# A different order of steps around the values of an attention kernel, with two of three key tiles of exponentials added on VectorE ahead of the sums

## The chip, the cores and the metric

The kernel runs on one core of one Trainium2 chip. The metric is the device time of one execution in microseconds (us), as the median of several executions. Every run also reports the core's span (first to last instruction; the quoted time is 1.8 us more in most runs, up to 3 in some) and the mean clock that was granted to TensorE, as a share of full speed. Engines are named as in the profile: PE is TensorE, PEld its weight loads, DVE is VectorE, ACT is ScalarE, POOL is GpSimd.

## The reference

A grouped-query attention (8 batches, 16 query heads on 4 key/value heads, 384 positions, head size 64) feeds a gated feed-forward layer whose gate is mixed over the positions:

```python
k, v = repeat(k, 4), repeat(v, 4)                  # 4 query heads share one key/value head
attn = exp(q @ k.T / 8 - max); attn = attn / attn.sum(-1)
x    = (attn @ v) -> [8, 384, 1024]
h    = maximum(x @ w_in, 0)                        # w_in [1024, 1024]
u, v = h[..., :512], h[..., 512:]
v_n  = (v - mean(v)) / sqrt(var(v) + 1e-6)
v_s  = einsum('ts,bsd->btd', w_spatial, v_n) + b_spatial
out  = (u * v_s) @ w_out                           # w_out [512, 1024]
```

## The kernel before

A batch is cut into small steps. The order in which the program issues them is the order in which each engine works. I use these short names, which are also those of the new code: `s` scores of one pair of PSUM banks (two matmuls of 512 columns), `e` their exps on ACT, `m` the sums of the exps (matmuls against a block of ones), `r` a reciprocal on ACT (`Ln`, then `Exp` of the negative), `x` the values (attention times v), `n` their normalisation on DVE, `V` the gate's v half with its relu on DVE, `S` its statistics on DVE, `rs` and `vn` the layer norm on ACT and DVE, `p` the mix over positions, `U` the u half with the gating on DVE, `O` one out chunk, copied out of PSUM by DVE. A prime counts batches back: `O0''` is an out chunk of two batches ago. `C0` and `C1` are the two values steps of a batch: 2 sums, 2 reciprocals, 4 values, 4 normalisations each. "Burst s9" below is the group of three score pairs s9, s10, s11, and so on.

PSUM has eight banks, and the one that was freed longest ago is taken next. A score burst needs three pairs, so six of the eight:

```python
    def take1():
        x = min((i for i in range(8) if not busy[i]), key=lambda i: used[i])
        ...
    def take2():
        x = min((i for i in range(0, 8, 2) if not busy[i] and not busy[i + 1]),
                key=lambda i: (max(used[i], used[i + 1]), min(used[i], used[i + 1])))
        ...
    def tiles(dst, a, quad, weights):
        for t in range(NST):                       # 3 key tiles
            for i in range(4):                     # 4 column groups of 32
                half, j = i // 2, quad * 2 + i % 2
                nc.tensor.matmul(dst[32 * i : 32 * (i + 1), :], weights(t, half),
                                 a[:, t, half, j * S : (j + 1) * S],
                                 start=(t == 0), stop=(t == NST - 1))

    def sums(b, gp, quad):
        x = take1()
        tiles(f32(x, S), T["aT", b, gp], quad, lambda t, half: ones32)
        T["sum", b, gp, quad] = x

    def norm(b, gp, quad, jj):
        ...
        nc.vector.tensor_tensor(T["xT", b][:, gp * 4 + quad * 2 + jj, :],
                                f32(x, S), T["rec", b, gp, quad], ALU.mult)
        touch(x)                                   # the bank is free after this

    def project(b, i, split=1):                    # O: one out chunk
        ...
        x = take1()
        pe_group(banks[:, x, :], ...)              # 4 matmuls
        nc.vector.tensor_copy(osb[:, half * 512 : (half + 1) * 512], banks[:, x, :])
        touch(x)
```

The steady order is made of six visits per batch:

```python
    def visit(b, vi):
        us = [3 * vi, 3 * vi + 1, 3 * vi + 2]
        ...                                        # score(u) x3, expo(u) for the first two
        if vi == 1 and b > 1:
            C(b - 1, 1, (0, 1))
        if vi == 4 and b < B:
            C(b, 0, (0, 1))
        ...                                        # expo of the third
        f, g = b - 1, b - 2
        run(*{
            0: [("sp", g, 2), ("U", g, 2), ("sp", g, 3), ("U", g, 3)],
            1: [("O", g, 0)],
            2: [("V", f, 0), ("st", f, 0), ("O", g, 1), ("V", f, 1), ("st", f, 1)],
            3: [("O", g, 2), ("V", f, 2), ("st", f, 2), ("O", g, 3), ("rs", f, 0), ("vn", f, 0)],
            4: [("O", g, 4)],
            5: [("O", g, 5), ("sp", f, 0), ("U", f, 0), ("sp", f, 1), ("U", f, 1)],
        }[vi])
        ...                                        # loads, casts and turns of the next batch
```

The softmax here doesn't subtract the row's maximum and nothing guards it: scores larger than these inputs give would overflow.

Of the kernel before, what the change touches and what calls it, by code (L numbers as in the profile page):

```python
# [17 lines left out]
def kernel(  # L18
# [73 lines left out]
    def take2():  # L92
        x = min(
            (i for i in range(0, 8, 2) if not busy[i] and not busy[i + 1]),
            key=lambda i: (max(used[i], used[i + 1]), min(used[i], used[i + 1])),
        )
        mark(True, (x, x + 1))
        return x
# [162 lines left out]
    def score(b, u):  # L261
# [3 lines left out]
        x = take2()  # L265
        rhs = T["qT", b, gp].rearrange("p j t q -> p (j t q)")
        for half in range(2):
            lo, hi = half * D, (half + 1) * D
            nc.tensor.matmul(  # L269
                banks[:, x + half, :],  # L270
# [5 lines left out]
        T["sc", b, u] = x  # L276

    def expo(b, u):
        gp, c, t = u // 9, (u % 9) // 3, u % 3
        x = T["sc", b, u]  # L280
        nc.scalar.activation(  # L281
            T["aT", b, gp][:, t, :, c * 512 : (c + 1) * 512], banks[:, x : x + 2, :], AF.Exp, scale=scale
        )
        touch(x, x + 1)

    def tiles(dst, a, quad, weights):
        for t in range(NST):
            for i in range(4):
# [3 lines left out]
                    weights(t, half),  # L292
                    a[:, t, half, j * S : (j + 1) * S],
                    start=(t == 0),
                    stop=(t == NST - 1),
                )

    def sums(b, gp, quad):
        x = take1()
        tiles(f32(x, S), T["aT", b, gp], quad, lambda t, half: ones32)  # L300
# [10 lines left out]
    def value(b, gp, quad, jj):  # L311
        v16 = T["v16", b]
# [3 lines left out]
            T["aT", b, gp],  # L316
            quad,
            lambda t, half: v16[:, 2 * gp + half, t, 32 * jj : 32 * (jj + 1)],
# [29 lines left out]
    def v_half(b, st):  # L348
        x = v_mm(b, st, range(4))
        part = ff.tile([P, DH], FP32, name=f"vpart_{st}", tag=f"vpart_{st}", bufs=1)  # L350
# [4 lines left out]
    def u_half(b, mu):  # L355
        x = u_mm(b, mu, range(4))
        part = ff.tile([P, S], FP32, name=f"upart_{mu}", tag=f"upart_{mu}", bufs=1)
# [4 lines left out]
    def gate_v(b, st):  # L362
# [3 lines left out]
        if part is None:  # L366
            if V_ON_ACT:
                nc.scalar.activation(v_r, banks[:, x, :], AF.Relu)
            else:
                nc.vector.tensor_scalar(v_r, banks[:, x, :], 0.0, None, op0=ALU.max)  # L370
# [86 lines left out]
    V_ON_ACT = False  # L457

    def ff_item(it):
        kind, b, i = it  # L460
        if b < 0 or b >= B:
            return
        {
            "V": gate_v, "st": stats, "sp": spatial, "U": gate_u, "O": project,
            "VA": v_half, "UA": u_half,
            "rs": lambda b, i: rstd(b), "vn": lambda b, i: v_norm(b, nc.vector),
        }[kind](b, i)


    def run(*items):  # L470
        for it in items:
            ff_item(it)

    def C(b, gp, quads):
        for qd in quads:
            sums(b, gp, qd)
        for qd in quads:
            recip(b, gp, qd)
        for qd in quads:
            for jj in range(2):  # L480
                value(b, gp, qd, jj)
                norm(b, gp, qd, jj)

    def visit(b, vi):
        us = [3 * vi, 3 * vi + 1, 3 * vi + 2]
        done = b == 1 and vi == 0
        if b < B and not done:
            for u in us:
                score(b, u)
            for u in us[:2]:  # L490
                expo(b, u)
        if vi == 1 and b > 1:
            C(b - 1, 1, (0, 1))
        if vi == 4 and b < B:
            C(b, 0, (0, 1))
        if b < B and not done:
            expo(b, us[2])
        f, g = b - 1, b - 2
        run(*{
            0: [("sp", g, 2), ("U", g, 2), ("sp", g, 3), ("U", g, 3)],  # L500
            1: [("O", g, 0)],
            2: [("V", f, 0), ("st", f, 0), ("O", g, 1), ("V", f, 1), ("st", f, 1)],
            3: [("O", g, 2), ("V", f, 2), ("st", f, 2), ("O", g, 3), ("rs", f, 0), ("vn", f, 0)],
            4: [("O", g, 4)],
            5: [("O", g, 5), ("sp", f, 0), ("U", f, 0), ("sp", f, 1), ("U", f, 1)],
        }[vi])
        n = b + 1
        if 2 <= n < B:
            if vi == 0:
                load_k(n)  # L510
                load_q(n, 0)
                load_v(n)
                load_q(n, 1)
            if vi == 1:
                cast_k(n, pool)
                for qd in range(2):
                    cast_q(n, 0, pool, 0, qd)
                    cast_q(n, 0, pool, 1, qd)
            if vi == 2:
                turn_k_dma(n)  # L520
                turn_q_dma(n, 0)
                for qd in range(2):
                    cast_q(n, 1, pool, 0, qd)
                    cast_q(n, 1, pool, 1, qd)
                cast_v(n, pool)
            if vi == 3:
                turn_q_dma(n, 1)

    with tc.manual_schedule():
        load_k(0, (0,))  # L530
        load_q(0, 0, (0,))
        load_q(0, 0, (1,))
        load_v(0)
        load_k(0, (1,))
        load_q(0, 1, (0,))
        load_q(0, 1, (1,))
# [4 lines left out]

        cast_k(0, vec, (0,))
        cast_q(0, 0, vec, 0, 0)
        cast_q(0, 0, pool, 1, 0)
        turn_k_pe(0, 0, act)
        turn_q_pe(0, 0, (0,), vec)
# [93 lines left out]
        for b in range(1, B):  # L640
            for vi in range(6):
                visit(b, vi)
# [39 lines left out]
```

## Time and profile before

| | before |
|---|---|
| median of the 3 runs known before the prediction | 272.46 us |
| the profiled run | 271.68 us, span 269.9 us, clock 1.00 |
| one steady batch (period) | 30.35 us, of which DVE works 18.1 and ACT 21.0 |

The prediction shows the lines that carry the argument. One view is added here, the waits of before (who waited on which line for whom: total us, times, longest):

```profile
ACT aT L281 <- PE banks L269: 44.2, 27, 3.0
DVE xT L326 <- ACT rec L308: 31.3, 17, 2.7
...
ACT rstd L388 <- DVE mv L384: 24.1, 8, 10.6
...
PE banks L290 <- ACT aT L281: 3.1, 7, 1.8
```

ACT waits for scores, DVE waits for reciprocals, and ACT waits for V2's statistics before `rs`. Idle time of an engine that is not the busiest costs nothing by itself, but it can make something late that PE needs, such as the normalisations, whose banks the next burst takes. Only the last line is a wait of PE, the engine that is nearly always busy. It is small because most of PE's waiting hides inside groups that the profile counts as busy. That is why all sizes below are differences of starts: a burst's start to the start of the next group, 0.75 us when undisturbed; what exceeds 0.75 I call its loss.

### The profile page before, as it was taken

The page shows a single profiled execution, that of the slowest core. Times are in us where ns is not written, and L with a number is a line of the kernel's source. Part 1 is how long each engine was busy: PE and PEld are TensorE (multiplying, and loading weights), DVE is VectorE, ACT ScalarE, POOL GpSimd, SP SyncE. Part 2 cuts the span into 40 slices and gives each one's busy share as a digit, 9 for nine tenths or more (in the row PEclk, how much of TensorE's full clock was granted, in tenths as well). Part 3 has the DMA queues.
Part 4 walks back from the last instruction along what each step waited for, and adds up shares of the span by engine and source line. Part 5 has one row for each costly group of instructions (what it writes and reads, how often), then busy time and mean ns, then how long its engine had stood idle before and what let it go on. Part 6 is the DMA issues. An engine that isn't in the chain of part 4 may idle for free.

```text
span 269.9 us, 5476 instructions
## 1 busy us (share of the span) xinstructions
PE 251.7 (93%) x2236; PEld 115.6 (43%) x2236; DVE 160.6 (60%) x309; ACT 171.2 (63%) x227; POOL 53.6 (20%) x100
## 2 busy tenths in 40 slices
PE   1799987799999999999999999999999999999994
PEld 1242432354345444454345444454345444454451
DVE  2424638685765466645765466635765566667964
ACT  2877987988495766577495766577595866520000
POOL 3639605343002500043002500043000000000000
PEclk9999999999999999999999999999999999999999
DMA  7999999890678529590868529490651021200415
GB/s 213 251 309 285 169 179 296 149 323 10 165 138 265 165 87 175 131 330 12 169 136 263 167 87 188 120 334 9 165 138 78 1 80 78 80 0 2 167 66 233
DMA packets 56921, 41.93 MB, mean 155 GB/s; under 512 B 26305, under 2 KB 53057, under 8 KB 56897
## 3 DMA queue, kind: packets, MB, share of 16 engines
q1 hardware_dynamic: 54048, 38.44, 52.6%
q0 software_dynamic: 2848, 3.15, 7.5%
q8 instruction: 17, 0.28, 0.5%
q14 instruction: 8, 0.06, 0.1%
HBM read 25.95 MB, written 12.58 MB: 143 GB/s over the span
## 4 chain that ended last, share of the span: by engine, by line
PE 73%; ACT 11%; DVE 10%; issue 3%; DMA 1%; POOL 0%; SPq 0%; DVEq 0%
PE banks L109 49%; PE banks L269 12%; PE banks L290 10%; ACT aT L281 6%; DVE xT L326 4%; DVE bn L383 2%; PE banks L250 2%; ACT rec L308 2%; DVE v_r L370 2%; DMA q<-in_q_dram 1%; ACT rec L306 1%; ACT rstd L388 1%; DVE v_r L372 1%; DVE mv L384 1%; ACT rstd L389 1%
## 5 line engine op out<-in xcount | busy, mean ns | idle before, releaser
L281 ACT ACTIVATE aT<-banks 128x1024 f16<-128x1024 f32 x144 | 137.8, 1023 | 44.7 <-PE banks L269 44.2
L269 PE MATMUL banks<-qT,kT 64*128 64x512 f16 x288 | 50.3, 393 | 3.5 <-ACT aT L281 1.0
L326 DVE TENSOR_TENSOR xT<-banks,rec 128x384 f16<-128x384 f32 x64 | 31.6, 552 | 33.3 <-ACT rec L308 31.3
L109 PE MATMUL banks<-w_out,gT 128*128 128x512 f16 x192 | 48.6, 380 | 0.0
L109 PE MATMUL banks<-xT,w_in 128*128 128x384 f16 x256 | 47.4, 326 | 0.0
L109 PE MATMUL banks<-w_in,xT 128*128 128x512 f16 x192 | 46.0, 380 | 1.2 <-DVE xT L326 0.6
L290 PE MATMUL banks<-aT,v 128*32 128x384 f16 x768 | 35.4, 332 | 3.1 <-ACT aT L281 3.1
L446 DVE COPY osb<-banks 128x512 f32<-128x512 f32 x48 | 32.5, 680 | 8.2 <-PE banks L109 8.1
L200 POOL CAST q<-q 128x384 f16<-128x384 f32 x57 | 28.0, 521 | 22.9 <-DMA q<-in_q_dram 20.7
L109 PEld LDWEIGHTS <-w_in 128*128 128x128 f16 x256 | 24.6, 98 | 17.1 <-issue 1.2
L109 PEld LDWEIGHTS <-xT 128*128 128x128 f16 x192 | 17.9, 98 | 25.4 <-issue 4.2
L290 PEld LDWEIGHTS <-v 128*32 128x32 f16 x768 | 22.1, 98 | 14.4 <-issue 5.8
L109 PEld LDWEIGHTS <-gT 128*128 128x128 f16 x192 | 16.7, 98 | 26.3 <-issue 8.9
L370 DVE TENSOR_SCALAR v_r<-banks 128x512 f32<-128x512 f32 x21 | 14.5, 692 | 22.0 <-PE banks L109 21.1
L269 PEld LDWEIGHTS <-kT 64*128 64x128 f16 x288 | 12.4, 94 | 35.0 <-issue 30.4
L176 POOL CAST k<-k 128x768 f16<-128x768 f32 x7 | 5.8, 827 | 108.4 <-DMA k<-in_k_dram 103.0
L427 DVE SCALAR_TENSOR_TENSOR gT<-banks,vs 128x384 f16<-128x384 f32 x28 | 15.6, 558 | 18.8 <-PE banks L109 18.8
L290 PE MATMUL banks<-aT,ones 128*32 128x384 f16 x384 | 20.6, 334 | 0.6
L109 PE MATMUL banks<-wsT,v_n 128*128 128x384 f16 x96 | 20.9, 327 | 0.0
L414 DVE TENSOR_TENSOR vs<-banks,bias_tp 128x384 f32<-128x384 f32 x32 | 17.6, 552 | 5.2 <-PE banks L109 4.8
L306 ACT ACTIVATE rec<-banks 128x384 f32<-128x384 f32 x32 | 15.5, 485 | 6.0 <-DVE vs L414 5.5
L388 ACT ACTIVATE rstd<-mv,eps_t 128x3 f32<-128x3 f32 x8 | 2.4, 297 | 24.1 <-DVE mv L384 24.1
(38 smaller groups left out, 123.9 us busy)
## 6 DMA issues: line engine op xcount, KB each, us to landing
q<-in_q_dram SPq DMA_DIRECT2D x32, 384.0 KB, 6.7
out_dram<-osb SPq DMA_DIRECT2D x23, 512.0 KB, 2.9
v<-in_v_dram SPq DMA_DIRECT2D x8, 384.0 KB, 5.9
k<-in_k_dram SPq DMA_DIRECT2D x7, 384.0 KB, 4.1
w_in<-in_moe_w_in_dram POOLq DMA_DIRECT2D x16, 128.0 KB, 6.0
w_out<-in_moe_w_out_dram POOLq DMA_DIRECT2D x2, 512.0 KB, 8.6
ws<-in_moe_w_spatial_dram SPq DMA_DIRECT2D x1, 576.0 KB, 8.7
out_dram<-osb SPq DMA_DIRECT2D x2, 256.0 KB, 2.4
```

Source lines behind the costliest of these rows:

```text
L109: nc.tensor.matmul(dst, w, m, start=(i == 0), stop=(i == n - 1))
L176: engine(T["k16", b][:, :, g0:g1, :], T["k32", b][:, g0:g1, :].rearrange("p g (t d) -> p t g d", t=NST),)
L200: engine(T["q16", b, gp][:, 2 * qd : 2 * qd + 2, :, half, :], T["q32", b, gp][:, qd, 2 * half : 2 * half + 2, :].rearrange("p j (t d) -> p ...
L269: nc.tensor.matmul(banks[:, x + half, :], T["kT", b][lo:hi, t, gp, :], rhs[lo:hi, c * 512 : (c + 1) * 512], start=True, stop=True,)
L281: nc.scalar.activation(T["aT", b, gp][:, t, :, c * 512 : (c + 1) * 512], banks[:, x : x + 2, :], AF.Exp, scale=scale)
L290: nc.tensor.matmul(dst[32 * i : 32 * (i + 1), :], weights(t, half), a[:, t, half, j * S : (j + 1) * S], start=(t == 0), stop=(t == NST - 1),)
L306: nc.scalar.activation(rec, f32(x, S), AF.Ln)
L326: nc.vector.tensor_tensor(T["xT", b][:, gp * 4 + quad * 2 + jj, :], f32(x, S), T["rec", b, gp, quad], ALU.mult)
L370: nc.vector.tensor_scalar(v_r, banks[:, x, :], 0.0, None, op0=ALU.max)
L414: nc.vector.tensor_tensor(vs, f32(x, S), bias_tp, ALU.add)
L427: nc.vector.scalar_tensor_tensor(T["gT", b][:, mu, :], src, 0.0, T["vs", b, mu], op0=ALU.max, op1=ALU.mult)
L446: nc.vector.tensor_copy(osb[:, half * 512 : (half + 1) * 512], banks[:, x, :])
```

## The change

The intent: two out chunks stand ahead of each values step, so that the exps and banks which the sums and values need are ready. The order ahead of C1 and C0 thus is burst, two out chunks, values step, burst. All four mix/gate steps `p U` of a batch stand in the two visits behind C0. And DVE adds two of the three key tiles of exps (fp16) before the sums, so that a sum streams two operands in place of three through PE. The adds are issued only from batch 2 on. The diff, cut to its core (the start-up is the same order in the new notation; buffers of partial results are merged so that the new tile `sT` has room):

```diff
+    def add(b, gp, c):
+        aT = T["aT", b, gp]
+        ...
+        cs = slice(c * 512, (c + 1) * 512)
+        nc.vector.tensor_tensor(T["sT", b, gp][:, :, cs], aT[:, 0, :, cs], aT[:, 1, :, cs], ALU.add)
+
     def sums(b, gp, quad):
         x = take1()
-        tiles(f32(x, S), T["aT", b, gp], quad, lambda t, half: ones32)
+        aT, sT = T["aT", b, gp], T.get(("sT", b, gp))
+        parts = [aT[:, t] for t in range(NST)] if sT is None else [sT, aT[:, 2]]
+        tiles(f32(x, S), quad, [(ones32, a) for a in parts])
...
-    def visit(b, vi):
-    ...
+    C1 = "m10' m11' r10' r11' x100' n100' x101' n101' x110' n110' x111' n111'"
+    C0 = "m00 m01 r00 r01 x000 n000 x001 n001 x010 n010 x011 n011"
+    VISITS = [
+        "s0 s1 s2 e0 e1 e2 a12' O0'' O1'' lk+ lq0+ lv+ lq1+", C1,
+        "s3 s4 s5 e3 e4 e5 V0' S0' V1' S1' a00 a01 ck+ cq0+",
+        "s6 s7 s8 e6 e7 e8 V2' S2' O2'' O3'' tk+ tq0+ cq1+ cv+",
+        "s9 s10 s11 e9 e10 e11 a02 O4'' rs' O5'' vn' tq1+", C0,
+        "s12 s13 s14 e12 e13 e14 p0' U0' p1' U1' a10",
+        "s15 s16 s17 e15 e16 e17 p2' U2' p3' U3' a11",
+    ]
...
+        for b in range(2, B):
+            play(b, STEADY if b > 2 else " ".join(w for w in STEADY.split() if w != "a12'"))
+        play(B, LAST)
```

`a` is an add, `l` a load, `c` a cast on POOL, `t` a turn (transposition) by DMA, and a plus counts batches ahead. In the same notation the order before was:

```text
s0 s1 s2 e0 e1 e2 p2'' U2'' p3'' U3''
s3 s4 s5 e3 e4 C1 e5 O0''
s6 s7 s8 e6 e7 e8 V0' S0' O1'' V1' S1'
s9 s10 s11 e9 e10 e11 O2'' V2' S2' O3'' rs' vn'
s12 s13 s14 e12 e13 C0 e14 O4''
s15 s16 s17 e15 e16 e17 O5'' p0' U0' p1' U1'
```

## The prediction

> **What bounds the kernel now.** I read the page first (engine shares, then slices), then the windows of one batch, then its timeline on TensorE (PE), then VectorE (DVE) around the places where PE stands still.
>
> From the page: PE is busy almost throughout, no other engine is close, and the granted clock is full, so the span is PE's time plus PE's holes.
>
> ```profile
> PE 251.7 (93%) x2236; PEld 115.6 (43%) x2236; DVE 160.6 (60%) x309; ACT 171.2 (63%) x227; POOL 53.6 (20%) x100
> ```
>
> The windows of three steady batches show a repeating period of 30.35 us. DVE works 18.1 us of it and ScalarE (ACT) 21.0 us:
>
> ```profile
> 109.40:139.75 30.35, 29.94 (x273) 13.80 (x272) 17.99 (x35) 21.00 (x29) 5.43 (x10) 1.00 0.65 169
> 139.75:170.10 30.35, 29.95 (x272) 13.80 (x272) 18.09 (x35) 21.00 (x29) 5.43 (x10) 1.00 0.65 163
> 170.10:200.46 30.36, 29.95 (x272) 13.77 (x272) 18.10 (x35) 21.01 (x29) 5.43 (x10) 1.00 0.59 163
> ```
>
> "Busy" hides waiting inside a group, so I take starts, not durations, from PE's timeline (start, length, engine, line, operation):
>
> ```profile
> 149.25 0.82 PE L269 MATMUL banks<-qT,kT 64*128 64x512 f16 x6
> 150.00 1.16 PE L290 MATMUL banks<-aT,ones 128*32 128x384 f16 x24
> 150.99 2.12 PE L290 MATMUL banks<-aT,v 128*32 128x384 f16 x48
> 153.04 1.04 PE L109 MATMUL banks<-w_out,gT 128*128 128x512 f16 x4
> 154.01 1.18 PE L269 MATMUL banks<-qT,kT 64*128 64x512 f16 x6
> 155.12 1.90 PE L109 MATMUL banks<-w_in,xT 128*128 128x512 f16 x8
> ...
> 164.61 1.44 PE L290 MATMUL banks<-aT,ones 128*32 128x384 f16 x24
> 166.27 2.13 PE L290 MATMUL banks<-aT,v 128*32 128x384 f16 x48 [0.22 <-ACT aT L281]
> 168.33 1.04 PE L109 MATMUL banks<-w_out,gT 128*128 128x512 f16 x4
> 169.30 1.39 PE L269 MATMUL banks<-qT,kT 64*128 64x512 f16 x6
> 170.62 0.60 PE L109 MATMUL banks<-w_out,gT 128*128 128x512 f16 x2
> ```
>
> An undisturbed score burst takes 150.00-149.25 = 0.75 us. The burst right after a values step takes 155.12-154.01 = 1.11 or 170.62-169.30 = 1.32, though one out chunk lies between. The sums take 0.99 us undisturbed, but 166.27-164.61 = 1.66 when the exps that they read (and the banks of the values) are late. So a batch loses 0.36+0.57+0.67 = 1.6 us of 30.35 to three stalls. Everything else, started one after the other, is 28.75 us of issue.
>
> The stalls are PSUM banks: the burst's third pair starts only when the last normalisation (xT, four at a 0.49 us pitch) is out.
>
> ```profile
> 168.09 1.96 DVE L326 TENSOR_TENSOR xT<-banks,rec 128x384 f16<-128x384 f32 x4 [1.30 <-ACT rec L308]
> 170.11 0.10 PEld L269 LDWEIGHTS <-kT 64*128 64x128 f16 x2 [0.37 <-issue]
> ```
>
> 168.09+1.96 = 170.05, and the last two weight loads follow at 170.11. The next group starts 0.57 us after that normalisation ends.
>
> **What the Trainium skill says.** "VectorE: DVE Perf Modes", section on the perf-mode tier table: tensor_tensor with all operands 16-bit in SBUF gets two elements a cycle, with a PSUM or fp32 operand one; the errata section there gives (N+151)/0.96 ns. The trace agrees at one per cycle: 384 elements give 557 ns by it, measured 552. The new add (1024 fp16 elements, all SBUF) has no row in the trace, so I estimate (512+151)/0.96 = 690 ns from that page; successive DVE operations start about 0.06 us before the former's recorded end (norms: 552 ns long, 0.49 pitch), so 0.63 us each.
> "TensorEngine Tiling (Array Packing)", Key Properties: a change of tiling mode drains the array. The trace shows about 0.1 us at each: an out chunk takes 0.87 us before another 128-column group and 0.97 before a score burst.
> "SBUF — State Buffer", Who interferes with whom: a DVE op with two SBUF inputs and a GpSimd op that reads SBUF exclude each other. No row of before shows it for tensor_tensor.
>
> **The change part by part.** The ramp is the same order. Only from batch 2 on are adds issued, so batches 0 and 1 keep three streams per sum.
>
> 1. *Sums.* Per batch four sums of 12 matmuls become 8. 24 take 0.99 us, so 16 take 0.66: 2 x 0.33 = 0.66 us less per batch, on the path. The total is 24 sums x 4 = 96 matmuls, and the built kernels do differ by 192 PE rows (matmul and weight load).
>
> 2. *Adds.* Six of about 0.63 us per batch, 36 in all: 3.8 us more DVE work per batch, 18.1 to 21.9 of about 29. DVE does not become the bound, but it becomes tight locally.
>
> 3. *Order.* There were 14 mode changes per batch (six score bursts, two values steps) and there still are. Only the pairs differ (out to values, values to scores), so I book nothing. Unstalled, the period is 28.75-0.66 = 28.1 us. The old stalls go: two out chunks (0.87+0.96) let three exps end (0.92 pitch) before the values need their banks, and the score burst after C1 needs n101 at 5.7 us and has it at 5.35.
>
> 4. *New stalls.* I walked one batch by hand from the start of its first burst, with trace durations (PE to DVE 0.2 us; relu with statistics 1.55; copy 0.66; norm and v_n 0.49) and the banks that the least-recently-used rule gives.
> - Burst s9 to s11: the third pair takes the banks of V2 and O2. V2 ends on PE at 12.1. DVE has relu and statistics of V1 from 9.75 to 11.3, adds a00 and a01 to 12.56, V2 with statistics to 14.1, O2's copy to 14.78. PE wants the pair at 14.33. With the 0.57 us of restart, the next group starts at 15.35 instead of 14.66: 0.69 us lost, most of it owed to the two adds.
> - C0 then starts at 17.2. DVE has a02, O4, O5 (to 18.06), v_n x3 (to 19.5), then the norms at 20.0, 20.5, 21.0, 21.5. Burst s12 to s14 starts at 19.9, and its third pair needs the second norm, 20.5: the next group comes at 21.08 instead of 20.64, 0.44 us lost. p0 and U0 then find their banks free within 0.05.
> - ACT ends the last exp of each burst before PE wants the bank everywhere; I find at least 1 us of slack except at the reciprocals of C0, about 0.1.
> Together 1.13 us, so the period is 28.1+1.1 = 29.2 us, against 30.35.
>
> 5. *Edges.* Before, batch 2's first burst starts at 55.1, the tail (after the last burst's sp and U) at 235.8, and the span ends at 269.9: 180.7 + 34.1. After: batch 1 now holds also p2 U2 p3 U3 of batch 0 in half form (4 x about 0.57 = 2.3 us), but it waits on exps (PE idles 1.82 us at 48.5, and ACT waits 1.85 us for statistics at 47.0). With V2 moved ahead of the third burst both shrink; I walk it to 54.5 instead of 55.1. Batches 2 to 7 are 6 x 29.2 + 0.3 (batch 2 has one values step without adds) = 175.5. The tail loses the gates moved out (3.6 us) and 0.33, and gains about 1 us, because only three out chunks (2.6 us), not four and more, cover the chain from V2's statistics over rstd to v_n: 31.1. Sum 54.5+175.5+31.1 = 261.1 us of span, 8.8 less than 269.9, so 272.46-8.8 = 263.7 us.
>
> **The rivals.**
> - *DVE takes the place of the wait.* If the adds ran at one element a cycle (1.22 us), DVE would gain 3.5 us a batch more, the s11 stall would grow by 1.1 and C0's chain by about 0.5: period 30.8, gain gone, about 272. For: the two stalls in my walk are both DVE's, and POOL casts can hold an add up for up to 0.5 us (the casts fall 4 to 13 us after a load's issue, which brushes a02). Against: fp16, unit stride, SBUF on all three sides.
> - *No new stall.* If DVE's queue is shorter than I booked, only PE's work is left: 28.1 a batch, 257 us. Against: DVE's order is fixed, and V2's and O2's evictions stand behind two adds.
> - *Only the matmuls count.* If the new order merely exchanged stalls one for one, 24 sums x 0.165 = 4.0 us would be all: 268.5.
> - *ACT binds.* 21.0 us of 29.2 with no queueing in my walk; only if reciprocals in C0 slip does s13 wait. A few tenths a batch.
>
> **Range and chances.** 263.7 us; each 0.3 us per batch of missed stall is 1.8 us in six batches. The no-new-stall rival sets the low side (257, unlikely), the one-for-one exchange the high side (268.5). I take 259.0 to 268.5. The 2% border is 267.0, which needs about 0.55 us a batch beyond my walk. Faster by over 2%: 0.80; within 2%: 0.18; slower: 0.02.
>
> **What would show it.** PE matmul count down by 96; the ones groups 16 long, 0.66 us. A period between 28.8 and 29.7. Six DVE adds a batch near 0.69 us each (1.2 would mean I am wrong on the mode). The bursts before O4 and after C0 longer than 0.75 us with the third pair's loads late, after osb's copy and after xT's norm. No stall in the first sums of C1. Batch 2's first burst near 54.5. I am wrong if the period is under 28.5 or the stalls sit in front of an exp.

## More of the kernel before

ACT's timeline around C0, in the batch whose PE lines the prediction shows:

```profile
164.77 0.30 ACT L388 ACTIVATE rstd<-mv,eps_t 128x3 f32<-128x3 f32 x1 [1.94 <-DVE mv L384]
165.10 0.20 ACT L389 ACTIVATE rstd<-rstd 128x3 f32<-128x3 f32 x1
165.21 1.92 ACT L281 ACTIVATE aT<-banks 128x1024 f16<-128x1024 f32 x2
```

The burst ahead of C0 starts at 163.86, but its exps start only at 165.21, since `rs` stands ahead of them and ACT was idle for 1.94 us before it. The values of C0, which need the banks of these exps, start at 166.27.

## The result, and the profile after

| | before | after |
|---|---|---|
| median (lowest to highest of 4 runs) | 272.22 us (271.84 to 272.48) | 262.01 us (261.42 to 264.03) |
| ratio, 95% interval | 1 | 0.9639 (0.9585 to 0.9693) |
| the profiled run | 271.68 us, span 269.9 | 262.19 us, span 260.4 |

The outputs are correct. A ratio here and below is the mean time of one kernel's runs over the mean of the other's of the same rounds, so it is not quite the ratio of the medians in the table. Executions over 1.5% slower than the fastest of the same kernel are left out of the means.

The page of the changed kernel, its engine line and the group of the adds (busy us, mean ns; then idle time before them):

```profile
PE 242.8 (93%) x2140; PEld 110.8 (43%) x2140; DVE 186.5 (72%) x345; ACT 172.6 (66%) x227; POOL 58.4 (22%) x100
...
L304 DVE TENSOR_TENSOR sT<-aT 128x1024 f16<-128x1024 f16 x36 | 26.6, 765 | 0.0
```

PE has 96 matmuls fewer, DVE 36 adds more. PE's share stays at 93%: the span shrank with its work. The mean of an add, 765 ns, hides a wide spread: the shortest took 657 ns, the median 683, the longest 1315.

Waits of the changed kernel:

```profile
DVE xT L338 <- ACT rec L318: 12.3, 10, 2.7
...
PE banks L269 <- DVE osb L459: 2.0, 4, 1.0
```

The normalisations wait 12.3 us in all for reciprocals where they waited 31.3. PE's wait for exps ahead of sums and values is gone from the list. In its place stands a wait of the scores for the copy of an out chunk.

Three batches in the view of windows (length, then busy us with instruction count of PE, PEld, DVE, ACT, POOL, the granted clock, DMA share, GB/s):

```profile
84.58:113.25 28.67, 28.58 (x258) 13.09 (x258) 21.84 (x40) 21.14 (x28) 6.26 (x10) 1.00 0.65 173
113.25:142.30 29.05, 28.52 (x257) 13.06 (x257) 22.47 (x40) 21.24 (x28) 6.67 (x10) 1.00 0.68 171
171.17:200.76 29.59, 28.54 (x257) 13.08 (x256) 22.92 (x40) 21.24 (x28) 5.91 (x10) 1.00 0.63 168
```

Unlike before, the batches differ: 28.67, 29.05 and 29.59 us for the same instructions. DVE's busy time grows along with the period, 21.84 to 22.92, at an equal count, so its instructions were stretched.

PE in the first of these batches (timeline: start, length, engine, line, operation):

```profile
98.50 1.17 PE L269 MATMUL banks<-qT,kT 64*128 64x512 f16 x6
99.60 1.90 PE L109 MATMUL banks<-w_out,gT 128*128 128x512 f16 x8
101.43 0.35 PE L291 MATMUL banks<-sT,ones 128*32 128x384 f16 x4
...
102.09 2.12 PE L291 MATMUL banks<-aT,v 128*32 128x384 f16 x48
104.15 0.91 PE L269 MATMUL banks<-qT,kT 64*128 64x512 f16 x6
105.14 0.65 PE L109 MATMUL banks<-wsT,v_n 128*128 128x384 f16 x3
```

The two sums take 102.09-101.43 = 0.66 us, without a hole before the values. Burst s9 takes 99.60-98.50 = 1.10 (a loss of 0.35), the burst after C0 105.14-104.15 = 0.99 (0.24). That was batch 3 (batches are counted from 0; the windows above are batches 3, 4 and 6). In batch 6 burst s9 looks so:

```profile
185.10 0.82 PE L269 MATMUL banks<-qT,kT 64*128 64x512 f16 x5
186.87 0.37 PE L269 MATMUL banks<-qT,kT 64*128 64x512 f16 x1 [0.96 <-DVE osb L459]
187.18 0.60 PE L109 MATMUL banks<-w_out,gT 128*128 128x512 f16 x2
```

It takes 187.18-185.10 = 2.08, a loss of 1.33. Its sixth matmul waits for the bank of O2, which DVE copies out. DVE's timeline in batch 3 (first line) and then in batch 6 shows what came ahead of that copy:

```profile
95.85 1.26 DVE L304 TENSOR_TENSOR sT<-aT 128x1024 f16<-128x1024 f16 x2
...
182.44 1.89 DVE L304 TENSOR_TENSOR sT<-aT 128x1024 f16<-128x1024 f16 x2
184.26 0.68 DVE L383 TENSOR_SCALAR v_r<-banks 128x512 f32<-128x512 f32 x1
...
186.13 1.29 DVE L459 COPY osb<-banks 128x512 f32<-128x512 f32 x2 [0.25 <-PE banks L269]
```

The same pair of adds, a00 and a01, took 1.26 us in one batch and 1.89 in the other. POOL's timeline at that moment of batch 6 (the second line is the second of the two casts alone), and then of batch 3:

```profile
182.38 1.42 POOL L200 CAST q<-q 128x384 f16<-128x384 f32 x2 [0.16 <-DMA q<-in_q_dram]
182.83 0.97 POOL L200 CAST q<-q 128x384 f16<-128x384 f32 x1
...
96.46 1.01 POOL L200 CAST q<-q 128x384 f16<-128x384 f32 x1 [0.69 <-DMA q<-in_q_dram]
```

Casts of q lie beside the adds in both batches, and whichever instruction starts later is stretched. In batch 6 the first cast began ahead of the adds and took its usual 0.51 us; the second began during the first add and took 0.97. In batch 3 the adds began first (95.85 and 96.42) and kept 0.66 and 0.68 us; the cast took 1.01. The whole trace agrees. The 21 adds with no cast beside them took at most 0.69 us, and so did the 3 that began ahead of the cast that they met. The 11 adds of 0.72 to 1.31 us all began while a cast ran, and each ended 0.54 us after the last such cast. (One more began 0.13 us before the end of a cast and kept 0.68 us.) Each cast of q that began during an add ended 0.37 us after that add. Over the batches the loss of burst s9 follows the length of the pair:

| batch | 2 | 3 | 4 | 5 | 6 | 7 |
|---|---|---|---|---|---|---|
| period, us | 29.56 | 28.67 | 29.05 | 28.87 | 29.59 | 28.59 |
| a00 and a01 together, us | 1.63 | 1.26 | 1.75 | 1.56 | 1.89 | 1.26 |
| loss of burst s9, us | 0.70 | 0.35 | 0.84 | 0.65 | 1.33 | 0.35 |
| loss of the burst after C0, us | 0.14 | 0.24 | 0.15 | 0.14 | 0.18 | 0.25 |

In all batches but 6, each 0.1 us that the pair is longer is about 0.1 us more loss (0.49 us longer and 0.49 more lost in batch 4 than in batch 3). Batch 6 lost 0.35 more than that, of which 0.25 is the wait of the copy in the last DVE line; why the copy waited there I could not find. The same copy waits in batch 6 of after_again and of e6, so it is not chance.

### The profile page after: what moved, and what is told of

Read it like the earlier page. It is cut to its first block, busy times and chain, and to the rows that moved or that the text cites. A ratio compares the mean times of both kernels' runs of the same rounds, so it can differ in the third digit from the quotient of the medians.

```text
span 260.4 us, 5301 instructions
## 1 busy us (share of the span) xinstructions
PE 242.8 (93%) x2140; PEld 110.8 (43%) x2140; DVE 186.5 (72%) x345; ACT 172.6 (66%) x227; POOL 58.4 (22%) x100
## 4 chain that ended last, share of the span: by engine, by line
PE 67%; DVE 18%; DMA 4%; ACT 4%; issue 3%; SPq 2%; POOL 0%; DVEq 0%
PE banks L109 46%; PE banks L269 10%; PE banks L291 9%; DMA q<-in_q_dram 4%; DVE xT L338 4%; DVE v_n L407 3%; DVE osb L459 3%; ACT aT L281 3%; PE banks L250 2%; DVE sT L304 2%; DVE bn L396 1%; DVE v_r L383 1%; DVE vs L427 1%; DVE uparts L438 1%; SPq L170 1%
## 5 line engine op out<-in xcount | busy, mean ns | idle before, releaser
L269 PE MATMUL banks<-qT,kT 64*128 64x512 f16 x288 | 46.7, 393 | 5.7 <-DVE osb L459 2.0
L109 PE MATMUL banks<-w_out,gT 128*128 128x512 f16 x192 | 45.7, 380 | 0.1
L109 PE MATMUL banks<-w_in,xT 128*128 128x512 f16 x192 | 45.1, 380 | 0.7 <-DVE xT L338 0.6
L338 DVE TENSOR_TENSOR xT<-banks,rec 128x384 f16<-128x384 f32 x64 | 31.4, 549 | 14.3 <-ACT rec L318 12.3
L200 POOL CAST q<-q 128x384 f16<-128x384 f32 x57 | 31.8, 587 | 16.3 <-DMA q<-in_q_dram 12.7
L109 PEld LDWEIGHTS <-gT 128*128 128x128 f16 x192 | 17.5, 98 | 29.8 <-issue 9.3
L304 DVE TENSOR_TENSOR sT<-aT 128x1024 f16<-128x1024 f16 x36 | 26.6, 765 | 0.0
L291 PEld LDWEIGHTS <-v 128*32 128x32 f16 x768 | 21.1, 99 | 11.0 <-issue 0.9
L383 DVE TENSOR_SCALAR v_r<-banks 128x512 f32<-128x512 f32 x21 | 14.4, 688 | 12.9 <-PE banks L109 12.3
L269 PEld LDWEIGHTS <-kT 64*128 64x128 f16 x288 | 10.9, 95 | 28.9 <-issue 23.1
L318 ACT ACTIVATE rec<-rec 128x384 f32<-128x384 f32 x32 | 16.7, 523 | 1.0
```

The costliest lines, as they stand in the source:

```text
L109: nc.tensor.matmul(dst, w, m, start=(i == 0), stop=(i == n - 1))
L200: engine(T["q16", b, gp][:, 2 * qd : 2 * qd + 2, :, half, :], T["q32", b, gp][:, qd, 2 * half : 2 * half + 2, :].rearrange("p j (t d) -> p ...
L269: nc.tensor.matmul(banks[:, xs[half], :], T["kT", b][lo:hi, t, gp, :], rhs[lo:hi, c * 512 : (c + 1) * 512], start=True, stop=True,)
L291: nc.tensor.matmul(dst[32 * i : 32 * (i + 1), :], weights if len(weights.shape) == 2 else weights[:, half, :], a[:, half, j * S : (j + 1) ...
L304: nc.vector.tensor_tensor(T["sT", b, gp][:, :, cs], aT[:, 0, :, cs], aT[:, 1, :, cs], ALU.add)
L318: nc.scalar.activation(rec, rec, AF.Exp, scale=-1.0)
```

## The experiments

All outputs were correct. Each kernel ran four times (a profile and three timed rounds) beside the kernel before on the same chip. The theory going in: the order gives most of the gain, the adds' 0.66 us a batch is eaten by stalls that they cause themselves on DVE. The rivals: the saved matmuls are the gain; or what limits is something other than DVE's queue. A remark that holds for all: the granted clock of many runs is about 0.99 since it dips for one to three fortieths of the span, most often during the start-up. In e3 such runs are longer by about 1.3 us and in e1 by 1.6 to 2.2; in the kernel before they are not (271.67 us at 0.993, 271.71 at 0.999 on one chip). So differences of less than about 2 us between kernels are read from the batches in the traces.

### e1: the new order without adds

```diff
     def play(b, text):
         for word in text.split():
             kind = word.rstrip("'+")
+            if kind[0] == "a":
+                continue
```

> The new order without any add; every sum again has three streams. My theory: the order alone already gives nearly all of the gain, because what the adds save on PE (0.66 us a batch) they give back at the third score pair of burst s9 to s11, where the profile of the changed kernel shows 0.35 to 1.33 us lost (mean 0.70 in batches 3 to 7). Without adds that loss falls to about 0.1 and the one after C0 from 0.19 to 0.1, so the period is 28.95+0.66-0.70 = 28.9 us and the time about 262 us, the same as with adds within 1 us (ratio to before 0.96). Rival (the adds' 96 matmuls come on top of the order's gain): 262+4 = 266 us, ratio 0.977.

Measured: 263.65 us (261.79 to 264.01), ratio 0.9667 (0.9629 to 0.9706). A batch took 29.00 us. PE at burst s9:

```profile
100.08 1.03 PE L269 MATMUL banks<-qT,kT 64*128 64x512 f16 x6
101.04 0.82 PE L109 MATMUL banks<-w_out,gT 128*128 128x512 f16 x3
```

The loss is 101.04-100.08-0.75 = 0.21, and 0.06 after C0. With the adds the means of batches 3 to 7 are 0.70 and 0.19. So the adds cost 0.62 us of new loss for 0.66 us of matmuls saved: 28.95 against 29.00 us a batch. In time the interval of e1 overlaps that of the full change: by the ratios the adds are worth 0.8 or 1.1 us (the change was measured twice), by the medians 1.6 or 1.8. But three of e1's four runs had the clock dip; its one run at 1.00 took 261.79 us, and the change's runs at 1.00 took 261.42 to 262.19. The order is nearly all of the gain, and "only the matmuls count" is wrong.

### e2 and e2b: the adds in the old order

In e2 the old order was played with the adds put in, and a02 stood behind `vn'` (only the new lines are shown):

```diff
+        "s0 s1 s2 e0 e1 e2 p2'' U2'' p3'' U3'' a12' ...",
+        "s3 s4 s5 e3 e4", C1, "e5 O0'' a00 ...",
+        "s6 s7 s8 e6 e7 e8 V0' S0' O1'' V1' S1' a01 ...",
+        "s9 s10 s11 e9 e10 e11 O2'' V2' S2' O3'' rs' vn' a02 ...",
+        "s12 s13 s14 e12 e13", C0, "e14 O4'' a10",
+        "s15 s16 s17 e15 e16 e17 O5'' p0' U0' p1' U1' a11",
```

> The old order with the same 36 adds, each put where VectorE is idle; 96 matmuls fewer. My theory: in the old order both values steps are followed by a wait on ScalarE (exps, then reciprocals, then norms), so PE only waits 0.33 us longer after each shorter sum: 271 to 272.5 us, no gain to speak of. Rival (the matmuls lie on the path wherever they are): 272.2-4.0 = 268.2 us, ratio 0.985.

Measured: 281.88 us (280.80 to 282.76), ratio 1.0349 (1.0316 to 1.0382). The waits of this kernel name the reason:

```profile
PE banks L291 <- DVE sT L304: 15.4, 9, 2.3
```

PE waited 15.4 us for the sums' new operand. The layer norm `vn'` waits for ACT behind three exps, and my a02 stood behind it in DVE's queue. This was my bad placement, and the run says nothing about adds in the old order. e2b moves the three adds to where DVE is idle (a12' behind `p2''`, a01 ahead of `V0'`, a02 between `O2''` and `V2'`):

```diff
-        "s0 ... p2'' U2'' p3'' U3'' a12' ...",     "... V0' S0' O1'' V1' S1' a01 ...",     "... O2'' V2' S2' O3'' rs' vn' a02 ...",
+        "s0 ... p2'' a12' U2'' p3'' U3'' ...",     "... a01 V0' S0' O1'' V1' S1' ...",     "... O2'' a02 V2' S2' O3'' rs' vn' ...",
```

> The old order with the adds once more, now each where VectorE had idle time in the profile of the kernel before: in the first try a02 stood behind v_n, which waits for rstd behind the exps, and PE waited 15.4 us for the adds over the run. Only the three adds a01, a02 and a12 have moved. My theory: 96 matmuls fewer in the old order buy next to nothing, since PE waits for exps and norms after each values step: 271 to 272.5 us. Rival (they lie on the path): 268.2 us.

Measured: 272.47 us (272.11 to 272.98), ratio 1.0004 (0.9969 to 1.0040): the same as before, though the 96 matmuls are gone here as well. A batch takes about 30.36 us, as before. PE's timeline at C0:

```profile
134.71 0.35 PE L291 MATMUL banks<-sT,ones 128*32 128x384 f16 x4
...
136.37 0.83 PE L291 MATMUL banks<-aT,v 128*32 128x384 f16 x16 [0.38 <-ACT aT L281]
```

From the sums to the values it is 136.37-134.71 = 1.66 us, exactly the 1.66 of before, although the sums themselves became 0.33 us shorter. Burst s6 behind C1 took 1.33 us where it took 1.11. Where the exps or the normalisations set the moment at which PE may go on, shorter sums only make PE wait longer. So the adds are worth nothing in the old order, and the new order is what could let them count.

### e3: two adds moved in DVE's queue

```diff
-        "s3 s4 s5 e3 e4 e5 V0' S0' V1' S1' a00 a01 ck+ cq0+",
-        "s6 s7 s8 e6 e7 e8 V2' S2' O2'' O3'' tk+ tq0+ cq1+ cv+",
+        "s3 s4 s5 e3 e4 e5 a00 V0' S0' V1' S1' a01 ck+ cq0+",
+        "s6 s7 s8 e6 e7 e8 V2' O2'' S2' O3'' tk+ tq0+ cq1+ cv+",
```

> The changed kernel with a00 ahead of V0, and O2's copy ahead of V2's statistics. My theory: the third pair of s9 to s11 no longer waits (loss 0.70 to under 0.1), but VectorE is full from V1 to the norms of C0, so the third pair of s12 to s14 waits longer (0.19 to about 0.6); net 0.2 to 0.3 us a batch, 260.5 us. Rival A (the s11 loss is simply gone): 262-4 = 258 us. Rival B (that loss is not VectorE's queue but banks held by ScalarE or a store): 262 us and the loss unchanged.

Measured: 261.13 us (260.36 to 261.77), ratio 0.9579 (0.9546 to 0.9612); a batch 28.67 us. PE at burst s9 and at the burst behind C0:

```profile
99.58 0.82 PE L269 MATMUL banks<-qT,kT 64*128 64x512 f16 x6
100.33 1.90 PE L109 MATMUL banks<-w_out,gT 128*128 128x512 f16 x8
...
104.88 1.25 PE L269 MATMUL banks<-qT,kT 64*128 64x512 f16 x6
106.22 0.65 PE L109 MATMUL banks<-wsT,v_n 128*128 128x384 f16 x3
```

Burst s9 takes 0.75 us: its loss is gone, by two moves in DVE's queue alone. Part of it came back: the burst behind C0 takes 106.22-104.88 = 1.34, a loss of 0.59 where the change has 0.19. S2, and with it the layer norm ahead of the normalisations, stands later in this order, which fits. The batch closes: 28.09+0.59 = 28.68. Some 0.3 us a batch remain as gain.

### e4: each add done twice

```diff
+        for _ in range(2):
             nc.vector.tensor_tensor(T["sT", b, gp][:, :, cs], aT[:, 0, :, cs], aT[:, 1, :, cs], ALU.add)
```

> The changed kernel with each add issued twice (same result). VectorE is 72% busy, so six more adds a batch (3.9 us) would fit into its idle time. My theory: only where they stand counts: two more adds ahead of V2's eviction add 1.3 us to the s11 loss, a12 twice delays the sums of C1 by about 0.4, a02 twice adds about 0.5 after C0: period 28.95+2.2 = 31.2 us, time about 275 us. Rival (VectorE has room): 262 to 264 us.

Measured: 281.26 us (278.64 to 283.32), ratio 1.0296 (1.0234 to 1.0358); the slowest run is left out of the ratio. The profile is of the fastest. PE at burst s9:

```profile
101.28 0.61 PE L269 MATMUL banks<-qT,kT 64*128 64x512 f16 x4
102.96 0.37 PE L269 MATMUL banks<-qT,kT 64*128 64x512 f16 x1 [1.07 <-DVE v_r L384]
104.49 0.37 PE L269 MATMUL banks<-qT,kT 64*128 64x512 f16 x1 [1.16 <-DVE osb L460]
```

The next group followed at 104.79: a loss of 2.76 us in this batch and of 2.48 on average over batches 3 to 7, where the change has 0.70. This is the strongest sign that DVE's queue sets this burst: four adds took 3.68 us (0.92 each, stretched) in place of two, and PE first waits for the relu of V2 and then for the copy of O2. I had expected a loss of about 2.0 and a time of 275; other waits of PE came along that I had not counted (6.9 us in all for copies, 4.4 for relus, 2.2 for the sums' operand), and the clock was as low as 0.973.

### e6: the casts of q moved away from the adds

The casts of POOL start when a load lands. Here, in the steady batches, the loads and the turns were issued two visits later, and the casts that were a visit ahead of the others were put with them:

```diff
-        "... a12' O0'' O1'' lk+ lq0+ lv+ lq1+", C1,   "... a00 a01 ck+ cq0+",   "... V2' S2' O2'' O3'' tk+ tq0+ cq1+ cv+",
-        "... vn' tq1+", C0,    "... U1' a10",                "... U3' a11",
+        "... a12' O0'' O1''", C1,   "... a00 a01",   "... V2' S2' O2'' O3'' lk+ lq0+ lq1+ lv+ ck+ cq0+ cq1+ cv+",
+        "... vn'", C0,         "... U1' a10 tk+ tq0+",       "... U3' a11 tq1+",
```

> The changed kernel with the loads of the next batch issued, and so cast by GpSimd, some 12 us later in each batch, away from the adds a00, a01 and a02. Theory: adds that overlap a GpSimd cast are stretched (up to 1.3 us against 0.68), which alone makes the s11 loss range from 0.35 to 1.33; with the casts away every add ahead of V2 takes at most 0.70 us and the loss is 0.35 in every batch: 2 us less in all, about 260 us. Rival (the spread comes from the stores or the loads themselves): spread unchanged, 262 us.

Measured: 275.23 us (272.67 to 277.49), ratio 1.0132 (1.0059 to 1.0205). No cast met a00, a01 or a02. All pairs a00 and a01 took 1.26 us, and burst s9 lost 0.33 to 0.35 us in all but one batch, which is what the change lost where its adds kept their length (the other was batch 6 again, with 0.70, with O2's copy waiting). The casts now met a10 and stretched it to 0.92 and 1.02 us in batches 3 and 4. But a new wait appeared, in the list of waits:

```profile
PE banks L269 <- DMA qT<-q: 10.4, 5, 2.5
```

The turned q of the next batch came too late: five batches began with 1.6 to 2.5 us of waiting. So the run agrees with casts that stretch the adds. The loads moved along with the casts, so it can't tell the two apart by itself; the ends of the adds above and the next run can. And it fails as a faster kernel for a reason that lies outside the question: my window for loads, casts and turns was too short.

### after_again: the change once more

No edit.

> The changed kernel itself on the same chip, for the comparison: 262 us, ratio to before 0.963. Its s11 losses again between 0.3 and 1.4 us; if they take other values in the same batches, they hang on when the loads land and not on the order.

Measured: 261.87 us (261.61 to 263.55), ratio 0.9627 (0.9583 to 0.9670). The pair a00, a01 took 1.61, 1.57, 1.26, 1.71, 1.79 and 1.26 us in batches 2 to 7. Burst s9 lost 0.68, 0.65, 0.35, 0.79, 1.23 and 0.35. Batch 4, stretched in the first profile, is undisturbed here, and batch 3 the other way round; in batch 7 no casts are left to meet, as there is no further batch. So in batches 3 and 4 it changes from one execution to the next whether an add or a cast starts first. POOL starts a cast when its load has landed, so the landing of the loads is the likely reason. Batch 4 also settles the rival of e6. This is the view of windows over its add a00:

```profile
126.26:126.92 0.66, 0.66 (x5) 0.31 (x4) 0.66 (x3) 0.66 (x2) 0.00 (x0) 1.00 1.11 333
```

No cast ran (POOL 0.00), the DMA engines moved 333 GB/s, as much as during the stretched pair of batch 6 of the first profile (338), and the add took 0.66 us. The traffic of loads and stores by itself doesn't stretch an add.

### e9: two out chunks beside each values step, all else in the old order, no adds

The diff is against the old order in the new notation.

```diff
-        "s3 s4 s5 e3 e4", C1, "e5 O0''",        "s6 s7 s8 e6 e7 e8 V0' S0' O1'' V1' S1'",
-        "s12 s13 s14 e12 e13", C0, "e14 O4''",  "s15 s16 s17 e15 e16 e17 O5'' p0' U0' p1' U1'",
+        "s3 s4 s5 e3 e4", C1, "e5 O0'' O1''",   "s6 s7 s8 e6 e7 e8 V0' S0' V1' S1'",
+        "s12 s13 s14 e12 e13", C0, "e14 O4'' O5''", "s15 s16 s17 e15 e16 e17 p0' U0' p1' U1'",
```

> The kernel before with one move only: O1 goes from between V0 and V1 to beside O0, and O5 from the next interval to beside O4, so that two out chunks, not one, lie between each values step and the next score burst. No adds, gates still split over two intervals, values step still right after a burst. Theory (balance): between two bursts ScalarE has three exps (2.85 us) and two reciprocals (2.0 us), 4.85 us, while PE had only 0.75+3.04+0.97 = 4.76 us there; with 0.87 us more PE work there both losses after the values steps (0.36 and 0.57 us) go, the one of 0.67 in front of C0's values stays: period 29.4 us, time about 266.5 us, ratio 0.979. Rival (it takes the values step moved behind the out chunks, or the gates in one stretch): 272 us.

Measured: 266.33 us (265.66 to 266.99), ratio 0.9790 (0.9767 to 0.9813); a batch 29.43 us. PE behind C1, then at C0:

```profile
122.85 0.82 PE L269 MATMUL banks<-qT,kT 64*128 64x512 f16 x6
123.61 0.60 PE L109 MATMUL banks<-w_in,xT 128*128 128x512 f16 x2
...
133.89 0.35 PE L291 MATMUL banks<-aT,v 128*32 128x384 f16 x4 [0.22 <-ACT aT L281]
```

The burst behind C1 takes 0.76 us, the one behind C0 0.75: with two out chunks (1.8 us of PE) between the values and the burst, the last normalisation is done in time. The wait inside C0 stays: the sums started at 132.23, so 133.89-132.23 = 1.66 us as before. `rs'` still stands ahead of the exps of burst s12 here, and ACT waits 1.94 us for V2's statistics as before. The arithmetic closes: 30.36-0.36-0.57 = 29.43. So 0.93 of the 1.36 us a batch that the order gains comes from simply having two out chunks beside a values step. The rest is the wait inside C0 (0.67) less the new losses of e1 (0.21 and 0.06): 0.40 of the 0.43 that are left.

### e8: the values step ahead of the two out chunks, no adds

```diff
-        "s0 s1 s2 e0 e1 e2 a12' O0'' O1'' ...", C1,
+        "s0 s1 s2 e0 e1 e2", C1, "O0'' O1'' ...",
-        "s9 s10 s11 e9 e10 e11 a02 O4'' rs' O5'' vn' tq1+", C0,
+        "s9 s10 s11 e9 e10 e11 rs' vn'", C0, "O4'' O5'' tq1+",
```

> The new order without adds (the run that gave 263.65), but with each values step in front of its two out chunks, right after the burst. Theory (balance): what matters is how much PE work shares the interval between two bursts with the reciprocals, not which comes first, so it stays within 2 us of 263.65. Rival (the values must come last so that the exps have ended and their banks are free): a wait in front of each values step and each second burst as before, 268 us or more.

Measured: 275.94 us (275.02 to 276.89), ratio 1.0144 (1.0114 to 1.0173). I had expected it within 2 us of e1, and it is 12 us slower. PE in C0 of batch 4, then DVE behind it:

```profile
134.85 1.16 PE L291 MATMUL banks<-aT,ones 128*32 128x384 f16 x24
135.83 2.12 PE L291 MATMUL banks<-aT,v 128*32 128x384 f16 x48
...
137.63 2.48 DVE L407 TENSOR_SCALAR v_n<-v_r,mv,rstd 128x512 f16<-128x512 f32 x3 [2.54 <-ACT rstd L402]
140.03 1.94 DVE L338 TENSOR_TENSOR xT<-banks,rec 128x384 f16<-128x384 f32 x4
141.89 1.27 DVE L459 COPY osb<-banks 128x512 f32<-128x512 f32 x2
```

The reciprocals and the layer norm's own ACT step stand behind three exps; DVE waits 2.54 us for the latter, then does layer norm, normalisations and only then the two copies. The burst that needs those banks takes 142.61-139.72 = 2.89 us (1.87 to 2.67 in batches 3 and 5 to 7). Behind C1, where no layer norm stands in DVE's queue, the burst takes 1.24 us. So it is not enough that the out chunks are in the interval. With the values last, ACT ends its exps and DVE its copies while PE does the out chunks. The run moves the layer norm and the copies together at C0, so it doesn't tell which of the two costs more there.

The run also shows what the prediction had not seen. Its sums take 135.83-134.85 = 0.98 us, so the old wait inside C0 is gone although no out chunk stands ahead of the sums. What differs from the old order there is ACT: V2 is a visit earlier, `rs'` stands behind the exps of the burst, and those start at 134.32, 0.43 us after their burst, where before it was 165.21-163.86 = 1.35. So the traces put that wait down to `rs'` ahead of the exps, and not to missing out chunks. No run moves `rs'` alone in the old order.

### e5 and e5_again: DVE's queue thinned out where it is tight

From e3 and e4: take O2's copy to ACT, put `rs'` earlier so that `vn'` comes ahead of O4 and O5 (the first batch keeps the change's order; in the tail V2 goes ahead of O2, and ACT copies O2 and O3):

```diff
-        "s3 s4 s5 e3 e4 e5 V0' S0' V1' S1' a00 a01 ck+ cq0+",
-        "s6 s7 s8 e6 e7 e8 V2' S2' O2'' O3'' tk+ tq0+ cq1+ cv+",
-        "s9 s10 s11 e9 e10 e11 a02 O4'' rs' O5'' vn' tq1+", C0,
+        "s3 s4 s5 e3 e4 e5 a00 V0' S0' V1' S1' a01 ck+ cq0+",
+        "s6 s7 s8 e6 e7 e8 V2' Oa2'' S2' rs' O3'' tk+ tq0+ cq1+ cv+",     # Oa: copied by ACT
+        "s9 s10 s11 e9 e10 e11 a02 vn' O4'' O5'' tq1+", C0,
```

> The changed kernel rebalanced for what the walk and the profile show as full: a00 ahead of V0, O2 evicted by ScalarE in its gap between two bursts, rstd right after V2's statistics, v_n ahead of O4's eviction, and in the tail V2 ahead of O2. Theory: both losses (s11 0.70, s12 to s14 0.19) fall under 0.1 each, period 28.95 to 28.1 or 28.3, and the tail loses 0.8 us: about 257 us, ratio to before 0.943. Rival (the next wait takes their place, ScalarE this time, because its copy and rstd push the exps): 260 us or more.

> The rebalanced kernel again: its profile had periods of 28.1 to 28.6 us, but its last store took 5 us where others take 2.4, and a dip of the granted clock in the ramp cost about 1.4. If these were chance, the span of some runs is near 256 us and the median near 258.5; if the store is always late, 259.5 again.

Measured: 259.52 us (258.61 to 261.07), ratio 0.9533 (0.9481 to 0.9585), and again on another chip 259.13 (257.38 to 259.82), ratio 0.9504 (0.9464 to 0.9544). The periods of batches 3 to 7 were 28.10, 28.28, 28.59, 28.10 and 28.1 us in the first profile, 28.23 on average and within the 28.1 to 28.3 expected; in the second those of batches 3 to 6 were 28.37 to 28.61. The loss of burst s9 is gone in all batches. That of the burst behind C0 is not under 0.1 as expected: it was 0 to 0.51 us in the first profile and 0.29 to 0.53 in batches 3 to 6 of the second. There the casts meet a02 and the layer norm: in batch 3 of the second profile the three operations of `vn'` took 0.72, 0.72 and 1.04 us, where they take 0.54 in batch 3 of the change. The time was 2 us over the 257 expected. In the profiled run of the first chip the tail was 32.0 us long in place of 31; its last two stores landed 4.4 and 4.1 us after their issue, where the change's took 2.5 and 2.3. The clock dipped in the start-up of both profiles. On the second chip the run with the clock at 1.00 took 257.38.

### e7: e5, and the casts a whole visit ahead of the adds

Loads are issued for two batches ahead, behind O5, and cast behind a10, so that no cast of q falls on a pair of adds that PE waits for:

```diff
-  ... "a12' O0'' O1'' lk+ lq0+ lv+ lq1+", C1,  "... S1' a01 ck+ cq0+",  "... rs' O3'' tk+ tq0+ cq1+ cv+",
-  ... "a02 vn' O4'' O5'' tq1+", C0,  "... U1' a10",
+  ... "a12' O0'' O1''", C1,  "... S1' a01 tk+ tq0+",  "... rs' O3'' tq1+",
+  ... "a02 vn' O4'' O5'' lk++ lq0++ lq1++ lv++", C0,  "... U1' a10 ck++ cq0++ cq1++ cv++",
```

> The rebalanced kernel with the loads of a batch issued a batch earlier, after O5's store, so that GpSimd casts fall in the stretch where VectorE has no add in a hurry, and the turned q is there in time (in the run with late casts it was not: PE waited 1.6 to 2.5 us for it in each batch). Theory: no add ahead of V2 or of the norms over 0.70 us, every period 28.1 us, about 0.7 us less than the rebalanced kernel. Rival (the earlier loads crowd out something else, a store or the first batches): the same or slower than it.

Measured: 256.56 us (255.90 to 258.50), ratio 0.9443 (0.9400 to 0.9486), the fastest of all by the median. (Its interval overlaps that of e5_again, 0.9464 to 0.9544, so the trace has to show the difference.) Two of its batches in the view of windows:

```profile
83.26:111.36 28.10, 28.10 (x259) 13.02 (x258) 21.64 (x39) 21.71 (x29) 6.61 (x11) 1.00 0.66 177
111.36:139.45 28.09, 28.09 (x257) 13.01 (x257) 21.75 (x39) 21.71 (x29) 6.57 (x11) 1.00 0.65 177
```

PE is busy for all of the batch, and all six bursts take 0.75 or 0.76 us in batches 2 to 7, the one behind C0 too. 28.1 us is the unstalled batch of the prediction. The casts still stretch adds, now a11 and a12' (1.58 to 1.82 us a pair in batches 2 to 5), where nothing waits for them. By the ratios e7 gains 1.7 or 2.4 us on e5 where 0.7 was expected. Part of that is the start-up, where e7's profile has no clock dip: batch 2 begins at 54.5 us, in e5 at 56.6 and 56.5.

### The ladder

By the ratios, times 272.2 us:

| kernel | ratio | us below before |
|---|---|---|
| e2b: adds alone, old order | 1.0004 | 0 |
| e9: two out chunks beside the values, no adds | 0.9790 | 5.7 |
| e1: the whole new order, no adds | 0.9667 | 9.1 |
| the change (two measurements) | 0.9639, 0.9627 | 9.8, 10.2 |
| e5: DVE's queue thinned out (two) | 0.9533, 0.9504 | 12.7, 13.5 |
| e7: casts moved out of the adds' way | 0.9443 | 15.2 |

Whether the adds bring their full 6 x 0.66 us in e7 was not tested: there is no run of e7 without adds. Nor does a run move the gates `p U` together and leave the rest of the old order.

## Why the prediction was right

The prediction was 263.7 us, the result 262.0, within the range, and faster by over 2% as said. Its steps:

1. *Sums.* Right: 96 matmuls fewer, and the ones groups take 0.66 us, 16 long.
2. *Adds.* Right in size: 683 ns median against 690 estimated, two undisturbed in 1.26 us against 2 x 0.63. (The pitch of 0.49 from which 0.63 came was misread: four normalisations in 1.96 us with a last one of 0.55 start (1.96-0.55)/3 = 0.47 apart. In batch 3 the second add starts 0.57 us after the first.) The rival "one element a cycle" is out. The cost beside POOL's casts was named as a risk of up to 0.5 us for a02. It fell on a02 as well (1.31 us in batch 6, 0.63 more than undisturbed) and on the pair a00 and a01 (up to 1.89-1.26 = 0.63), and only the pair's stretch shows in the losses.
3. *Order.* Right in size, wrong in one of its reasons. No old stall is left, and the mean period of batches 3 to 7, 28.95 us, less its two losses of 0.70 and 0.19 is 28.06 against 28.1; e7 ran at 28.10. e9 shows that two losses of the old order go by the two out chunks alone. The third, in C0, did not go because "two out chunks let three exps end": e8 has no out chunk there and no wait (0.98 us from sums to values). The exps were late because `rs` stood ahead of them on ACT and waited 1.94 us for V2's statistics, and the new order has V2 a visit earlier and `rs` behind the exps. That the order took this stall away was luck as far as the stated reason goes.
4. *New stalls.* The places were right, and the first size was right by two errors that cancelled. Burst s9: predicted 0.69, measured 0.70 on average. But that average is made of 0.35 in undisturbed batches and 0.65 to 1.33 in stretched ones. The walk's term that failed is the restart of 0.57 us. That was read where both matmuls of a pair waited; here only the last one waits. In batch 3 O2's copy ends at 99.24 and the next group starts at 99.60, in batch 6 at 186.82 and 187.18: 0.36 us each time. The copy also came 0.1 us earlier than walked. Both together make the 0.34 us too much in an undisturbed batch, and the stretching of the adds, which the walk left out, gave it back. "Most of it owed to the two adds" does not follow from the walk: V2 ends on PE at 12.1, so without adds DVE could take it at 12.3 and not at 12.56, and only 0.26 of the 0.69 are owed to them. Measured, it is 0.14 of 0.35 in undisturbed batches (0.21 remain in e1), and most of the loss only on average (0.49 of 0.70), because of the casts. Burst behind C0: predicted 0.44, measured 0.19, so this term was mis-sized by 0.25. In batch 3 the second normalisation ended about 0.47 us after the burst's start (walked: 0.60) and the next group came 0.52 us after it (walked: 0.58); batch 7 lost as much (0.25), the others 0.14 to 0.18.
5. *Edges.* Batch 2 started at 55.0 us (54.5), six batches took 174.3 (175.5), the tail 31.05 (31.1): the span was 260.4 against 261.1.

So of the miss of 1.7 us, six batches give 1.2, less 0.5 for the late start: 0.7. The rest is the last line of the sum: 272.46-8.8 took the difference of spans from the median of the runs, while the span of 269.9 belongs to a run of 271.68. Span plus 1.8 us would have been nearer: 261.1+1.8 = 262.9.

Of the rivals, the exchange of stalls one for one (268.5) is refuted by e1 and e2b: it is the stalls that went, and the matmuls that were nearly exchanged, one for one, for new losses of the adds. "DVE takes the wait's place" is true in kind (e4 shows how fast) and small in size.

## What to carry to other kernels

Count work saved on the busiest engine only where that engine sets the next start: the same 96 matmuls were worth nothing in the old order (the wait grew by as much) and nearly nothing in the new one as long as DVE's queue held the next burst up. With that queue cleared (e7) the batch came down to 28.10 us, the unstalled batch with the matmuls' full 0.66 off; a run of e7 without adds, which would prove it, is missing. Before moving work, follow each wait to its end: the exps that PE waited for were late because of an instruction ahead of them in ACT's queue, which itself waited. To remove a wait for a buffer, first put other work of the busy engine between the producer and the user, in an order in which the helper engines catch up meanwhile; then look at which copy stands last in their queue, and at what else on the chip can stretch that queue. Read losses from starts of groups, batch by batch: a mean that agrees with a forecast can be two errors.

## What the Trainium skill lacked or had wrong

- "SBUF — State Buffer", Who interferes with whom: the rule is right here (two-input DVE adds beside GpSimd casts), but it gives no size for `tensor_tensor`. Measured: an add of 128x1024 fp16 elements takes 0.66 to 0.69 us alone and up to 1.31 beside casts. The one that starts later pays: every stretched add began while a cast of q or v ran and ended 0.54 us after it, and a cast of q that began during an add ended 0.37 us after the add (0.81 to 1.01 us long in most cases, 0.51 alone).
- "VectorE: DVE Perf Modes", Terms: it says of the flush at the end of each operation that the next one can't issue until the pipe is empty. Read alone, this suggests that operations don't overlap; a later section of the page ("The DRAIN you can't avoid") says that an operation that isn't held starts earlier, without a figure. The recorded pitch of successive operations is shorter than their recorded length: two adds of 0.66 and 0.68 us in 1.26 us, four normalisations of 0.55 us in 1.94. Its duration formula for the add was within about 1% (690 ns against a median of 683).
- "TensorEngine Tiling (Array Packing)", Key Properties: the drain at a change of tiling mode has no figure. Here such a change comes with about 0.1 us (an out chunk takes 0.97 us ahead of a score burst, 0.87 ahead of a group of the same tiling).
- No page gives the time from the release of a PSUM bank by a DVE copy to the next group on PE: here 0.36 us when the last matmul of the burst waited. In the kernel before it was 0.57 from a normalisation, when the burst's last two matmuls waited.
